# The first chunk's block squarings, with units crossed between the column halves of the matmul array

## The chip, the core and the metric

The kernel runs on one core of a Trainium2 chip. Its engines work side by side, each through its own list of instructions in a fixed order: TensorE (PE, with its weight loads shown as PEld), VectorE (DVE), ScalarE (ACT), GpSimd (POOL) and SyncE (SP), which issues most DMAs. The metric is the device time of one execution in microseconds (us). Before the change three runs took 644.02, 644.89 and 645.16 us; the median is 644.89.

## What is computed

A recurrent attention block (RWKV7, 4 batches, 8 heads, 768 steps, head dimension 40) and behind it a feed-forward block with an exact GELU:

```python
for t in range(S):
    y[:, :, t] = np.einsum('bhd,bhde->bhe', rt, state)
    Sa = np.einsum('bhde,bhe->bhd', state, at)
    state_decay = state * wt[:, :, None, :] - np.einsum('bhd,bhe->bhde', Sa, bt)
    state = state_decay + np.einsum('bhd,bhe->bhde', vt, kt)
...
h = x @ w_in
g = 0.5 * h * (1.0 + erf(h * inv_sqrt2))
return g @ w_out
```

x is the attention's output, 3072 rows of 320; w_in is 320 x 2048 and w_out 2048 x 320, both given in 64 bits and turned into fp32 on the chip.

## The kernel before

The sequence is cut into 12 chunks of 64 steps. Within a chunk the recurrence becomes matrix products per head: N (from a and b), A, RV, M, and the inverse of (1 - N), with which the vectors sa of all 64 steps come out at once; the state is handed from chunk to chunk by new_state. The feed-forward block of a chunk (ph, gelu, po) follows some chunks later. All instructions are put down by hand, in one order per engine; there is no scheduler. Calls of the helper keep and warm put matmuls between a constant and the identity ahead of others, to keep PE busy.

The inverse of a 64 x 64 triangular matrix is made from its two 32 x 32 diagonal blocks and a corner. For chunks from the second on, the blocks are inverted by an elimination on POOL (eliminate: 31 steps of a multiply and an add). For chunk 0 they are inverted on PE: with Z the two diagonal blocks and T = 1 + Z, each step squares Z and adds Z² T to T, so that T = (1 + Z)(1 + Z²)(1 + Z⁴)... There are five steps, k = 0 to 4; step 0 only squares, step 4 only makes the last product for T.

A unit is one head of one batch; 16 units stand on the free axis for each half of the 128 partitions, so 32 units in all, each with two blocks. Z, T and Z's transpose ZT lie in SBUF, partition half q holding unit (q, m). square(k, h) multiplies the units m of half h (8 of them, for both partition halves): the matmul of unit (q, m) reads rows half(q) of the array and writes PSUM partitions half(q), that is columns half(q) of the array. One matmul of fp32 shows in the trace as two records. A step then needs, for each h: turn_square (DVE transposes the new Z out of PSUM into ZT), copy_square (ACT copies the new Z to SBUF) and add_square (DVE adds the product Z² T to T in SBUF). Z and T are parts of one SBUF tile called SM in the trace, ZT lies in the tile Nb. Two engines that read or write one PSUM tile are kept apart by semaphores, also where both only read.

Around the squarings, in each engine's order:

- POOL: start_T(0), scale_k(0), the preparation of chunk 1's elimination, then that elimination (its tiles are called st and spare_x).
- PE: square(0, ·), flip_r, flip_k (transposes of r and k; flip_k needs scale_k), square(1, ·), square(2, 0), make_A, square(2, 1), square(3, ·), flip_v, square(4, ·), make_av, make_RV, corner_direct (the product J), joined_direct, make_saT, make_sa, make_M, make_A of chunk 1, make_QY.
- DVE: the transposes and adds, and between them mask_A and parts of the conversion of the feed-forward weights (U[..].a, m, b).
- ACT: the copies, and between them copy_r, copy_k and copy_v; copy_v needs flip_v.

QY of chunk 0 gives the state after it (new_state, DVE) and the outputs (scale_y).

## Time and profile before

| | |
|---|---|
| median of three runs | 644.89 us |
| the profiled execution | 643.49 us, its span 641.8 us |
| PE busy | 624.2 us |
| DVE, ACT, POOL busy | 450.5, 373.5, 392.2 us |
| squares of chunk 0 | from 26.2 to 46.6 us |
| granted TensorE clock | 0.996 of full speed |

The page gives busy times of one execution; a row of a timeline has the start and the length in us, then engine, line, operation, the tile written and those read, the shape and the count of merged instructions. In brackets stands the idle time of the engine ahead of the row, and what ended it. "issue" is idle time that ended with nothing that the profile shows. A table by stage has, for each stretch, its length and the busy time of each engine. The chain of waits of the whole span goes 86% through PE, so that a delay of PE's early work counts as far as nothing later waits for something else.

### The profile page before, as it was taken

How to read it: one execution, taken by the hardware profiler on the slowest of the kernel's cores; microseconds unless marked ns; L12 is line 12 of the kernel's file. 1: busy time of each engine (PE TensorE's matmuls, PEld its weight loads, DVE VectorE, ACT ScalarE, POOL GpSimd, SP SyncE). 2: the span in 40 equal slices, each digit the busy share in tenths (PEclk: the TensorE clock that was granted, in tenths of full speed). 3: DMA queues.
4: the chain of work that ended last, by engine and by line, in shares of the span. 5: the costliest groups of instructions: out<-in, count | busy, mean ns of one | idle time of the engine just before them, and what ended most of it. 6: DMA issues, size and time to landing. Idle time of an engine off the chain costs nothing.

```text
span 641.8 us, 32951 instructions
## 1 busy us (share of the span) xinstructions
PE 624.2 (97%) x14788; PEld 553.9 (86%) x14788; DVE 450.5 (70%) x604; ACT 373.5 (58%) x717; POOL 392.2 (61%) x806
## 2 busy tenths in 40 slices
PE   6899899999999999999999999999999999999997
PEld 4787788787878899998998998988989989989977
DVE  1775889996467899685995995985987965623313
ACT  4437694664265479447487587576587687274020
POOL 7587478822857814898848858858758768620000
PEclk9999899999999999999999999999999999999999
DMA  9986767448234643465555466374465450210100
GB/s 139 176 143 138 131 137 164 104 106 149 60 75 75 117 99 67 94 113 120 111 105 100 95 116 115 74 130 86 80 120 106 84 98 5 43 25 10 35 2 21
DMA packets 227119, 60.47 MB, mean 94 GB/s; under 512 B 208603, under 2 KB 225275, under 8 KB 226978
## 3 DMA queue, kind: packets, MB, share of 16 engines
q1 hardware_dynamic: 225946, 56.33, 47.2%
q8 instruction: 116, 1.90, 1.3%
q0 software_dynamic: 592, 1.70, 1.2%
q10 hardware_dynamic: 440, 0.33, 0.2%
q14 instruction: 25, 0.20, 0.1%
HBM read 50.46 MB, written 3.93 MB: 85 GB/s over the span
## 4 chain that ended last, share of the span: by engine, by line
PE 86%; DVE 4%; POOL 3%; SPq 2%; DMA 2%; ACT 2%; issue 1%; ACTq 0%; DVEq 0%; POOLq 0%
PE ph L1414 33%; PE po L1317 22%; PE QY L139 7%; PE po L1424 5%; PE po L1250 2%; PE J L139 2%; PE N_ps L139 2%; PE RV_ps L139 2%; PE saT_ps L139 2%; PE M_ps L139 2%; POOL st L863 2%; POOL st L861 2%; PE A_ps L139 1%; PE X L139 1%; PE av L139 1%
## 5 line engine op out<-in xcount | busy, mean ns | idle before, releaser
L1414 PE MATMUL ph<-xt,w_in_sb 64*64 64x256 f32 (+1 forms) x3360 | 218.4, 377 | 1.9 <-issue 1.8
L1414 PEld LDWEIGHTS ph<-xt,w_in_sb 64*64 64x64 f32 (+1 forms) x3360 | 175.1, 141 | 30.1 <-DMA v_pairs<-in_v_dram 1.7
L861 POOL TENSOR_TENSOR tmp<-W,Nb 128x126 f32<-128x126 f32 (+22 forms) x310 | 129.5, 418 | 57.6 <-DVE Nb L876 34.1
L863 POOL TENSOR_TENSOR W<-W,tmp 128x126 f32<-128x126 f32 (+22 forms) x310 | 147.3, 475 | 24.3
L1418 ACT ACTIVATE gt<-ph 128x1024 f32<-128x1024 f32 x48 | 49.2, 1025 | 92.4 <-PE ph L1414 89.0
L1317 PE MATMUL po<-w_out_sb,gt 128*128 128x160 f32 x576 | 84.3, 302 | 0.0
L1317 PEld LDWEIGHTS po<-w_out_sb,gt 128*128 128x128 f32 x576 | 79.2, 190 | 1.2
L1218 ACT COPY turned<-within 8x64 f32<-8x64 f32 (+3 forms) x144 | 46.4, 322 | 3.5 <-DVE within L1207 1.6
L814 POOL TENSOR_TENSOR VR<-VR,upper 128x1024 f32<-128x1024 f32 x8 | 18.9, 2366 | 30.2 <-ACT VR L810 26.7
L580 ACT COPY part<-part 32x256 f32<-32x256 f32 (+1 forms) x112 | 36.1, 322 | 1.7
L1424 PE MATMUL po<-w_out_sb,gt 128*128 128x320 f32 x128 | 36.5, 438 | 0.5 <-DVE w_out_sb L386 0.5
L1092 DVE STREAM_TRANSPOSE sa<-saT 128x1024 f32<-128x1024 f32 x9 | 11.1, 1238 | 32.1 <-ACT saT L1079 32.1
L1101 ACT COPY SM<-sa 32x64 f32<-32x64 f32 (+1 forms) x108 | 31.8, 294 | 1.4
L1424 PEld LDWEIGHTS po<-w_out_sb,gt 128*128 128x128 f32 x128 | 23.7, 190 | 10.2 <-DVE w_out_sb L386 1.0
L1340 DVE TENSOR_TENSOR os<-os,po 128x160 f32<-128x160 f32 x63 | 19.7, 314 | 17.4 <-PE po L1317 10.5
L1337 ACT COPY os<-po 128x160 f32<-128x160 f32 x9 | 2.6, 290 | 41.9 <-PE po L1317 41.9
L376 ACT ACTIVATE conv<-conv,rebias 128x320 uint32<-128x320 uint32 (+1 forms) x26 | 15.8, 620 | 15.7 <-DVE conv L373 15.6
L1317 PE MATMUL po<-extra,half 128*128 128x160 f32 x160 | 23.2, 299 | 0.0
L876 DVE STREAM_TRANSPOSE Nb<-N 128x1024 f32<-128x1024 f32 x10 | 21.6, 2158 | 1.7 <-ACT N L798 1.7
L1035 DVE COPY Tt<-J 32x512 f32<-32x512 f32 x9 | 6.2, 689 | 23.2 <-PE J L139 23.2
L1317 PEld LDWEIGHTS po<-extra,half 128*128 128x128 f32 x160 | 22.2, 190 | 0.0
L1317 PE MATMUL po<-extra,gt 128*128 128x160 f32 x144 | 21.1, 300 | 0.0
(301 smaller groups left out, 1280.7 us busy)
## 6 DMA issues: line engine op xcount, KB each, us to landing
VR<-in_v_dram SPq DMA_DIRECT2D x24, 160.0 KB
out_dram<-os SPq DMA_DIRECT2D x45, 80.0 KB
b_rows<-in_b_dram SPq DMA_DIRECT2D x22, 160.0 KB
k_rows<-in_k_dram SPq DMA_DIRECT2D x22, 160.0 KB
a_pairs<-in_a_dram SPq DMA_DIRECT2D x18, 144.0 KB
v_pairs<-in_v_dram SPq DMA_DIRECT2D x36, 72.0 KB
r_pairs<-in_r_dram SPq DMA_DIRECT2D x36, 72.0 KB
a_pairs<-in_b_dram SPq DMA_DIRECT2D x16, 144.0 KB
```

The source lines that it names most:

```text
L139: nc.tensor.matmul(o, lhsT, rhs, start=first, stop=True, skip_group_check=True)
L580: nc.scalar.copy(to[at:at + BL, :, x, z * BL:end], tmp[on:on + BL, e, :, q * BL:q * BL + end - z * BL])
L861: eng.tensor_tensor(t, W[:, :rows, j:j + 1].to_broadcast([P, rows, rest]), Nb[:, j:j + 1, j + 1:].to_broadcast([P, rows, rest]), ALU.mult)
L863: eng.tensor_tensor(W[:, :rows, j + 1:], W[:, :rows, j + 1:], t, ALU.add)
L876: nc.vector.transpose(Nb.rearrange("p s t -> p t s"), N[:, :, :BL].rearrange("p n t -> p t n").unsqueeze(2).to_broadcast([P, BL, 2, NBL]))
L1101: copy(SM[to:to + BL, g].rearrange("p q m c -> p (q m) c")[:, :, d * BL:end], t["sa"][at:at + BL, :, to:to + end - d * BL])
L1218: nc.scalar.copy(tn[to:to + deep, :, at:at + wide], within[0][at:at + deep, :, to:to + wide])
L1317: nc.tensor.matmul(self.pt[at][:, n, :DM // 2], l_[:, f], r_[:, f], start=f == 0, stop=f == NF // 2 - 1)
L1340: nc.vector.tensor_tensor(to, one_, other, ALU.add)
L1414: nc.tensor.matmul(pt[to:end, x, s], w_in_sb[half(x), kt, p * P + to:p * P + end], xt[half(x), kt], start=kt == 0, stop=kt == NK - 1)
L1418: nc.scalar.activation(gt[:, 4 * q:4 * q + 4].rearrange("p (x s) t -> p x s t", x=2), phs.pop((c, q)), ACT.Gelu)
L1424: nc.tensor.matmul(pos[c][:, g], gt[:, f, g * P:(g + 1) * P], w_out_sb[:, f], start=f == 0, stop=f == NF - 1)
```

## The change

In square(k, h) with k below 4, odd units n of a half now write the other half of the columns: the matmul of unit (q, m) reads rows half(q) and writes half(1 - q). So an odd unit stands in the other partition half after every such step, and after four steps is back. Its product is laid out by n % 2 over the two PSUM banks of the tile instead of by n // 4. T must follow: start_T puts the odd units' T into the other half to begin with, in eight operations instead of four; add_square adds T from SBUF to the product in PSUM, one operation for the even units and one for each half of the odd ones; copy_square copies Z and T (96 columns instead of 64) to SBUF, behind the adds. In step 3, where no copy_square for Z is wanted, add_square itself has ACT copy T. In step 4 everything is as before. In the list of calls one add_square and one copy_square change places.

```diff
     def start_T(c, eng):
-        for rows, cols in quads:
-            eng.tensor_tensor(sq["T"][rows], sq["Z"][rows, :, cols], ident[rows, rows].unsqueeze(1).to_broadcast([BL, NBL, BL]),
-                              ALU.add)
+        for x in range(2):
+            for n, (rows, cols) in enumerate(quads):
+                to = quads[(n + 2 * x) % 4][0]
+                eng.tensor_tensor(sq["T"][to, x::2], sq["Z"][rows, x::2, cols],
+                                  ident[rows, rows].unsqueeze(1).to_broadcast([BL, NBL // 2, BL]), ALU.add)
 
     def square(k, h):
         at, end = 0 if k < 4 else HP, HP if k == 0 else 3 * BL
         pt = duo("sq", 2 * k + h)[:, :, :12 * BL].rearrange("p z (n t) -> p z n t", t=3 * BL)
-        sq["pt", h] = pt
+        sq["pt", h], sq["k", h] = pt, k
         for n in range(NBL // 2):
             for q in range(2):
-                m = h * NBL // 2 + n
-                mm(pt[half(q), n // 4, n % 4, at:end], sq["ZT"][half(q), m], sq["both"][half(q), m, at:end])
+                m, to = h * NBL // 2 + n, half(q ^ n % 2 if k < 4 else q)
+                mm(pt[to, n % 2, n // 2, at:end], sq["ZT"][half(q), m], sq["both"][half(q), m, at:end])
 
     def halves(t, h):
-        return t[:, h * NBL // 2:(h + 1) * NBL // 2].rearrange("p (z n) t -> p z n t", z=2)
+        return t[:, h * NBL // 2:(h + 1) * NBL // 2].rearrange("p (n z) t -> p z n t", z=2)
 
     def copy_square(h):
-        nc.scalar.copy(halves(sq["Z"], h), sq["pt", h][:, :, :, :HP])
+        end = 3 * BL if sq["k", h] else HP
+        nc.scalar.copy(halves(sq["both"], h)[:, :, :, :end], sq["pt", h][:, :, :, :end])
 
     def add_square(h):
-        T = halves(sq["T"], h)
-        nc.vector.tensor_tensor(T, T, sq["pt", h][:, :, :, HP:], ALU.add)
+        T, pt, k = halves(sq["T"], h), sq["pt", h][:, :, :, HP:], sq["k", h]
+        if k == 4:
+            nc.vector.tensor_tensor(T, T, pt, ALU.add)
+            return
+        nc.vector.tensor_tensor(pt[:, 0], T[:, 0], pt[:, 0], ALU.add)
+        for q in range(2):
+            nc.vector.tensor_tensor(pt[half(q), 1], T[half(1 - q), 1], pt[half(q), 1], ALU.add)
+        if k == 3:
+            nc.scalar.copy(T, pt)
...
     turn_square(1)
     load_w(2)
+    add_square(1)
     copy_square(1)
-    add_square(1)
     substitute(1, 8)
```

## Prediction, made before the changed kernel was run

> **What bounds the kernel now.** The page first, then the waits of the stretch behind the change, then a table by stage.

> ```profile
> span 641.8 us, 32951 instructions
> PE 624.2 (97%) x14788; PEld 553.9 (86%) x14788; DVE 450.5 (70%) x604; ACT 373.5 (58%) x717; POOL 392.2 (61%) x806
> ...
> DVE st L1187 <- PE QY L139: 2.7, 1, 2.7
> ...
> 70.00:80.00 10.00, 10.00 (x318) 7.99 (x317) 9.90 (x17) 6.86 (x10) 4.62 (x4) 0.98 0.49 116
> 80.00:90.00 10.00, 9.04 (x346) 7.84 (x346) 9.41 (x13) 9.55 (x16) 6.69 (x8) 1.00 0.48 125
> 90.00:130.00 40.00, 39.50 (x798) 32.97 (x795) 37.53 (x65) 23.79 (x32) 33.67 (x69) 1.00 0.65 137
> ```

> In the table by stage the third number is PE's busy time, then PEld, DVE, ACT, POOL. From 70 us on DVE (9.90 of 10, 9.41 of 10, 37.53 of 40) and then PE have no room; DVE came to that backlog after 2.7 us of waiting for QY of chunk 0 (matmuls that end near 69.7 us). So whatever moves that QY moves the end about one for one. QY hangs, in PE's fixed order, on the corner product J of chunk 0, and J on the block squarings: the change lies on the chain, though it touches only 26 to 50 us.

> **The matmuls alone.** From the timeline of PE (start, length, count):

> ```profile
> 25.18 1.16 PE L139 MATMUL N_ps<-aT,nT 40*64 40x64 f32 x64
> 26.16 2.03 PE L139 MATMUL sq<-SM,Nb 64*64 64x64 f32 x64
> 31.04 2.86 PE L139 MATMUL sq<-SM,Nb 64*64 64x96 f32 x64
> 44.51 2.00 PE L139 MATMUL sq<-SM,Nb 64*64 64x32 f32 x62
> 101.20 1.66 PE L139 MATMUL QY<-SM,extra 64*64 64x104 f32 x64
> ```

> N_ps is written in just the order of halves that the squares get (rows and columns 0/0, 1/1, 0/1, 1/0) and needs 1.16 us for 64 records of 64 columns; the squares of today, on 0/0 and 1/1 only, need 2.03. QY, on all four, needs 1.66 for 104 columns, the squares 2.86 for 96. I take 1.43 for a pair of squares with 96 columns, 0.71 for a half of it: 0.72 off each half, 1.0 off step 0, nothing off step 4, which isn't crossed. Bounds: 0 (no gain) and 0.72.

> **Ahead of the squares: POOL.**

> ```profile
> 23.08 5.25 POOL L931 TENSOR_TENSOR SM<-SM,ident 32x512 f32<-32x512 f32 x4 [9.54 <-ACT wpT L527]
> 28.41 1.56 POOL L626 TENSOR_TENSOR extra<-k_rows,part 128x640 f32<-128x640 f32 x1
> 30.02 0.86 PEld L587 LDWEIGHTS kT_ps<-ident,extra 128*128 128x128 f32 x8 [0.29 <-POOL extra L626]
> 31.29 0.24 POOL L861 TENSOR_TENSOR st<-st,spare_x 128x31 f32<-128x31 f32 x1 [0.45 <-DVE spare_x L876]
> 47.30 0.41 POOL L861 TENSOR_TENSOR st<-st,spare_x 128x126 f32<-128x126 f32 x1
> ```

> start_T goes from four operations of 512 elements (5.25/4 = 1.31 each) to eight of 256. Through 0.41 plus a gap of some 0.04 at 126 elements and 1.31 at 512, 256 cost 0.74: 5.9 us in all, +0.65; bounds 0 (cost by elements alone) and +1.3 (twice that). Four of them cross partitions, which no row shows; the upper bound is for that. scale_k follows on POOL, PE's kT transposes wait for it (the 0.29), and squares 1 follow these on PE. So step 0's gain of 1.0 is lost in that wait, and square(1,0) starts at 31.7 instead of 31.04. POOL's own elimination for chunk 1 had 0.45 to spare and starts 0.2 later; its result is turned on DVE behind masks that PE holds up anyway.

> **Inside the squares: DVE and ACT.**

> ```profile
> 32.63 0.72 DVE L947 STREAM_TRANSPOSE Nb<-sq 128x512 f32<-128x512 f32 x1 [1.49 <-PE sq L139]
> 33.27 0.38 DVE L954 TENSOR_TENSOR SM<-SM,sq 128x256 f32<-128x256 f32 x1
> 33.58 0.41 DVE L373 TENSOR_SCALAR conv<-w_out_sb 128x512 uint32<-128x512 uint32 x1
> 35.78 0.42 DVE L954 TENSOR_TENSOR SM<-SM,sq 128x256 f32<-128x256 f32 x1 [1.12 <-ACT SM L950]
> 37.06 1.21 DVE L755 TENSOR_TENSOR A<-A_ps,upper 128x1024 f32<-128x1024 f32 x1
> 39.26 0.41 DVE L954 TENSOR_TENSOR SM<-SM,sq 128x256 f32<-128x256 f32 x1
> 40.37 0.72 DVE L947 STREAM_TRANSPOSE Nb<-sq 128x512 f32<-128x512 f32 x1 [0.71 <-ACT SM L950]
> 41.32 0.42 DVE L954 TENSOR_TENSOR SM<-SM,sq 128x256 f32<-128x256 f32 x1 [0.23 <-PE sq L139]
> 41.66 0.71 DVE L947 STREAM_TRANSPOSE Nb<-sq 128x512 f32<-128x512 f32 x1
> 46.83 0.41 DVE L954 TENSOR_TENSOR SM<-SM,sq 128x256 f32<-128x256 f32 x1
> ...
> L1340 DVE TENSOR_TENSOR os<-os,po 128x160 f32<-128x160 f32 x63 | 19.7, 314 | 17.4 <-PE po L1317 10.5
> ...
> 33.76 0.58 ACT L950 COPY SM<-sq 128x512 f32<-128x512 f32 x1 [2.83 <-DVE SM L954]
> 39.76 0.58 ACT L950 COPY SM<-sq 128x512 f32<-128x512 f32 x1 [1.92 <-DVE SM L954]
> 44.63 1.01 ACT L727 COPY vT<-vT_ps 128x1024 f32<-128x1024 f32 x1 [4.29 <-PE vT_ps L139]
> 80.15 0.38 ACT L1009 COPY Js<-J 128x256 f32<-128x256 f32 x1
> ```

> An add of 256 elements takes 0.41, one of 160 takes 0.314: 1 ns per element and 0.15 fixed, so 128 take 0.28. Below step 4 each add becomes three of 128 elements, each waiting for the end of the one before (0.03): 0.93 for 0.41. Bounds 0.61 (half of 0.41 each, no gap) and 1.05 (0.314 each). No row has DVE writing to PSUM; the upper bound stands for it. ACT's copies grow from 64 to 96 columns: between 0.58 at 512 elements and 1.01 at 1024 (which are the bounds), 768 cost 0.80; and they must now wait for the adds. In step 3 ACT gets two new copies of T of 256 elements (0.38, as Js).

> Now the chain, before → after, each event started by the last thing it waits for:

> - Square(1,0) seen by DVE: 32.63 → 32.55 (31.7 + 0.71 + 0.15 to DVE).
> - DVE then runs without a pause: transpose 0.7, adds 0.93, the conversion 0.4, transpose, adds (36.25), transpose and adds of step 2 (37.95). mask_A, 37.06 → 37.95. The 1.12 that DVE waited for ACT are used up by it. Add(1) of step 2 follows the same conversions: 39.26 → 40.2, end 39.67 → 41.1.
> - Copy(1), 39.76 → 41.2, now 0.80: the transpose behind it 40.37 → 42.05.
> - Add(0) of step 3 stands behind that transpose on DVE: 41.32 → 42.8, end 43.75. Transpose(0) waits for the new copy of T (43.85 to 44.25), since two engines take turns at one PSUM tile: 41.66 → 44.3.
> - flip_v needs that transpose (its PSUM tile): 42.61 → 45.05, and copy_v 44.63 → 47.05. The copy of T(1) stands behind copy_v on ACT, 48.05 to 48.45; transpose(1) waits for it, ends 49.15, and square(4,1) starts then instead of 45.5 (half of the 2.00).
> - Behind the copy of T(1) ACT also holds the conversion of a weight unit, wanted on DVE only after add(1). Add(1) of step 4: 46.83 → 50.4. On PE av, RV and a warming matmul follow square(4,1), and J starts at 52.5 instead of 49.45.

> ```profile
> 42.61 1.97 PE L139 MATMUL vT_ps<-ident,VR 128*64 128x128 f32 x32
> 48.06 0.89 PEld L139 LDWEIGHTS RV_ps<-rT,vT 40*64 40x64 f32 x52 [0.45 <-issue]
> 49.45 1.20 PE L139 MATMUL J<-Nb,N 32*32 32x32 f32 x64
> 52.63 0.14 PEld L587 LDWEIGHTS rT_ps<-ident,v_pairs 128*128 128x128 f32 x1 [0.83 <-issue]
> 56.63 0.20 PEld L139 LDWEIGHTS saT_ps<-Tt,avs 64*64 64x64 f32 x7 [0.20 <-issue]
> 60.36 0.32 PEld L139 LDWEIGHTS M_ps<-rT,saT 40*64 40x64 f32 x15 [0.32 <-issue]
> 66.28 0.46 PEld L139 LDWEIGHTS QY<-SM,extra 64*64 64x64 f32 x18 [2.31 <-issue]
> ...
> q8 instruction: 116, 1.90, 1.3%
> ```

> So +3.05 us at J; the 0.45 in RV is used up in it. Had the adds cost 0.61, the same steps give +1.4 at J, because the new copy of T behind copy_v stays. What then lies between J and QY are the "issue" gaps. Queue 8, of kind instruction, moved 116 packets: 2 x 14788 instructions over them is 255 each, so 128 weight loads and 128 matmuls; and the gaps stand about 128 records apart (52 of RV, 2, 64 of J, 2, 7 of rT up to 52.63). [...] They go by when PE enters the block before, so most of the delay passes; with light DMA traffic at the new times I take 0.55 of the 0.83 and the smaller ones off: **+2.5 us at QY**, and at the end. The profiled execution took 643.49 (span 641.8 and 1.7 around it): 646.0. It lies 1.4 below the median of the runs, 644.89; on that the forecast is **647.4**.

> [...]

> **The rivals.**

> [...] Chance 0.22: 0.13 that it ends within 0.2%, 0.09 faster. [...]

> *The permuted transposes are slow* (slower still). One row stands for it:

> ```profile
> 62.62 1.12 DVE L892 STREAM_TRANSPOSE Nb<-st 128x512 f32<-128x512 f32 x1
> ```

> 1.12 instead of 0.71 for the same 512 elements, where the order is permuted finely; L949 keeps runs of 64, so I don't expect it; six transposes on the chain would add 2.4: 649.8. Chance 0.07.

> *The crossing gives PE nothing*: only square(1,0) is on the chain as a matmul, so +0.7: 648.1. N_ps speaks against it. Chance 0.06.

> **How the numbers follow.** My forecast (delay passes, 645.7 to 648.6 as adds and POOL go from bound to bound: +1.4 or +4.3 at J, less 0.55) has 0.65. Changes under 0.2% (1.3 us) can't be told from none. Slower: 0.65 + 0.07 + 0.06, less 0.02 for cheap adds within the forecast: 0.76. Same: 0.13 + 0.02 = 0.15. Faster 0.09. The range, 644.0 to 649.4, leaves out most of the faster half of the first rival and the slow transposes.

> **What would show it.** Squares 1 to 3 at 1.4 us per 64 records; three DVE operations of about 0.28 per add, DVE busy nearly without a pause from 32.5 to 41; ACT copies of 0.80; copy of T(1) behind copy_v; J near 52.5 and QY's second part near 68.8. Wrong: J at or before 49.5, or J late and QY at 66.3.

## The result, and the profile after

The changed kernel took 650.42 us (median of four runs: 646.82 to 653.02) against 644.45 us before (the three runs given above and a fourth of 641.05): ratio 1.011, 95% interval 1.0075 to 1.0146. In a second set of six runs (after_again below) it was 1.0103 (1.0065 to 1.0141). It is slower by about 1%, 6 us between the medians and 7 by the ratio, where +2.5 was forecast; the time lies outside the forecast range of 644.0 to 649.4.

The profiled execution after took 651.02 us. The page's span, and the table by stage (length, then busy time of PE, PEld, DVE, ACT and POOL, the granted TensorE clock, DMA share, GB/s):

```profile
span 649.3 us, 32970 instructions
```

```profile
10.00:20.00 10.00, 6.81 (x60) 5.35 (x64) 1.23 (x1) 5.78 (x6) 3.54 (x6) 0.81 1.27 186
20.00:26.00 6.00, 6.00 (x74) 5.88 (x67) 2.96 (x3) 1.08 (x2) 0.00 (x0) 0.50 1.18 144
...
32.00:40.00 8.00, 4.74 (x115) 3.97 (x113) 6.09 (x11) 4.49 (x7) 6.78 (x18) 1.00 1.02 177
40.00:47.00 7.00, 6.97 (x129) 4.99 (x128) 5.69 (x13) 2.45 (x4) 5.90 (x15) 0.51 0.89 124
...
70.00:80.00 10.00, 9.80 (x227) 8.49 (x229) 6.12 (x9) 5.33 (x10) 3.55 (x3) 0.66 0.11 20
```

The last number but two, the granted clock, had no term in the prediction: TensorE ran at half clock at 16 to 26, at 40 to 47 and at 71 to 78 us. The first of these lies ahead of every changed instruction on TensorE; the start of start_T on POOL, which nothing of the change precedes, moved from 23.08 to 26.45. So the chain has to be read from start_T on. From its timeline, one engine after the other:

```profile
26.45 6.20 POOL L933 TENSOR_TENSOR SM<-SM,ident 32x256 f32<-32x256 f32 x8 [12.92 <-ACT wpT L527]
35.35 1.55 PE L139 MATMUL sq<-SM,Nb 64*64 64x96 f32 x64
43.31 2.93 PE L139 MATMUL sq<-cum_m,ident 128*128 128x512 f32 x4
49.71 1.97 PE L139 MATMUL vT_ps<-ident,VR 128*64 128x128 f32 x32 [1.34 <-DVE Nb L949]
57.27 1.20 PE L139 MATMUL J<-Nb,N 32*32 32x32 f32 x64
...
36.31 0.72 DVE L949 STREAM_TRANSPOSE Nb<-sq 128x512 f32<-128x512 f32 x1 [1.25 <-PE sq L139]
37.13 0.30 DVE L960 TENSOR_TENSOR sq<-SM,sq 128x128 f32<-128x128 f32 x1
37.53 0.70 DVE L962 TENSOR_TENSOR sq<-SM,sq 64x128 f32<-64x128 f32 x2
38.33 0.43 DVE L373 TENSOR_SCALAR conv<-w_out_sb 128x512 uint32<-128x512 uint32 x1
...
44.80 0.29 DVE L960 TENSOR_TENSOR sq<-SM,sq 128x128 f32<-128x128 f32 x1
45.13 0.63 DVE L962 TENSOR_TENSOR sq<-SM,sq 64x128 f32<-64x128 f32 x2
46.70 0.72 DVE L949 STREAM_TRANSPOSE Nb<-sq 128x512 f32<-128x512 f32 x1 [0.94 <-ACT SM L953]
...
45.87 0.80 ACT L953 COPY SM<-sq 128x768 f32<-128x768 f32 x1 [2.58 <-DVE sq L962]
48.53 0.37 ACT L964 COPY SM<-sq 128x256 f32<-128x256 f32 x1 [1.86 <-DVE sq L962]
51.72 1.01 ACT L727 COPY vT<-vT_ps 128x1024 f32<-128x1024 f32 x1 [2.82 <-PE vT_ps L139]
52.63 0.38 ACT L964 COPY SM<-sq 128x256 f32<-128x256 f32 x1
```

What the crossing should do it does: 64 records of 96 columns fell from 2.86 to 1.55 us. What it costs is there too: eight operations of 0.775 on POOL, three sums in the place of one (37.13 to 38.23, later 44.80 to 45.76), copies of 0.80, and the copy of T(1) at 52.63, right behind copy_v. From the start of start_T to J is 57.27 - 26.45 = 30.82 us, and 49.45 - 23.08 = 26.37 before: **+4.45**, where the prediction had +3.05. This distance is used for all kernels below. In the first profile before it is 26.37; in four further profiles of kernels that leave the squarings as they were (before_again, before_warm_early, shift_24, shift_64) it is 25.88 to 26.44, so that a figure from one profile is good to about half a microsecond.

### The profile page after: what moved, and what is told of

Read it like the earlier page. It is cut to its first block, busy times and chain, and to the rows that moved or that the text cites. A ratio compares the mean times of both kernels' runs of the same rounds, so it can differ in the third digit from the quotient of the medians.

```text
span 649.3 us, 32970 instructions
## 1 busy us (share of the span) xinstructions
PE 627.5 (97%) x14788; PEld 555.5 (86%) x14788; DVE 453.4 (70%) x616; ACT 375.1 (58%) x719; POOL 395.7 (61%) x810
## 4 chain that ended last, share of the span: by engine, by line
PE 89%; DVE 3%; ACT 2%; issue 1%; POOL 1%; SPq 1%; DMA 1%; DVEq 0%; ACTq 0%; POOLq 0%
PE ph L1424 33%; PE po L1327 22%; PE QY L139 7%; PE po L1434 5%; PE J L139 3%; PE po L1260 2%; PE A_ps L139 2%; PE M_ps L139 2%; PE saT_ps L139 2%; PE N_ps L139 2%; PE RV_ps L139 2%; PE av L139 2%; PE X L139 1%; PE sq L139 1%; SPq L194 1%
## 5 line engine op out<-in xcount | busy, mean ns | idle before, releaser
L863 POOL TENSOR_TENSOR W<-W,tmp 128x126 f32<-128x126 f32 (+22 forms) x310 | 151.0, 487 | 24.3
L861 POOL TENSOR_TENSOR tmp<-W,Nb 128x126 f32<-128x126 f32 (+22 forms) x310 | 129.1, 416 | 57.4 <-DVE Nb L876 33.9
L1350 DVE TENSOR_TENSOR os<-os,po 128x160 f32<-128x160 f32 x63 | 19.7, 313 | 17.4 <-PE po L1327 10.5
L876 DVE STREAM_TRANSPOSE Nb<-N 128x1024 f32<-128x1024 f32 x10 | 21.6, 2156 | 1.7 <-ACT N L798 1.7
L755 DVE TENSOR_TENSOR SM<-M_ps,upper 128x1024 f32<-128x1024 f32 x12 | 14.7, 1223 | 11.4 <-PE M_ps L139 11.2
```

Source lines behind the costliest of these rows:

```text
L861: eng.tensor_tensor(t, W[:, :rows, j:j + 1].to_broadcast([P, rows, rest]), Nb[:, j:j + 1, j + 1:].to_broadcast([P, rows, rest]), ALU.mult)
L863: eng.tensor_tensor(W[:, :rows, j + 1:], W[:, :rows, j + 1:], t, ALU.add)
L876: nc.vector.transpose(Nb.rearrange("p s t -> p t s"), N[:, :, :BL].rearrange("p n t -> p t n").unsqueeze(2).to_broadcast([P, BL, 2, NBL]))
L1350: nc.vector.tensor_tensor(to, one_, other, ALU.add)
```

## The experiments

**Both kernels again, and the stretch ahead of the change.** before_again and after_again are the two kernels unchanged. The two others have four warming products more, ahead of cum of the second chunk:

```diff
+    warm(4, 4, 4, 4)
     sums_cum(1)
```

> The kernel before, unchanged, once more, for the spread of its time and of its granted clock. Theory (clock): the stretch of half clock at 15.4 to 25.7 us in the profile of the changed kernel (0.50 granted, wT_ps 128x128 x16 3.78 us against 2.05) stands ahead of every changed instruction, behind an idle TensorE stretch that both kernels have (3.0 us before cum, behind ACT wpT L527); so it is a matter of the execution and not of the change, and the kernel before has it in some executions too: its executions lie in two groups, near 641 to 642 us with a mean clock of 0.996 or more, and near 645 us with a clock of 0.988 to 0.99. Rival (the change makes it): the kernel before never has it; all its executions have a clock of 0.995 or more.

> The kernel before with four warming products of 512 columns (about 0.64 us each by the row of N_ps<-cum_m,ident 128x512, 2.6 us together) in the idle stretch of 3.0 us ahead of cum of the second chunk. Theory (clock): full clock at 15 to 26 us in every execution, 0 to 2 us faster than before (the early dip happens in some executions only), median 642.5 to 644.5. Rival: the dip never happens in the kernel before, so nothing is gained; 644.0 to 646.5, the warming products delaying cum by up to 0.5 us.

> The changed kernel with the same four warming products in the idle stretch ahead of cum of the second chunk, nothing else. Theory (clock): the half clock at 15 to 26 us is gone in every execution; the profile shows square(0) starting near 26.2 us as before and the time falls from 650.4 to 646.5 to 648; what is left over the kernel before, 2.5 to 4 us, is the crossing's own. Rival (the early half clock is a cause of nothing, or comes from the change by another way): 649.5 or more.

> The changed kernel, unchanged, beside the three others, to have more than four executions of it. Chain of sums and copies plus a clock that varies: 648 to 650 us, clocks from 0.982 to 0.992, and the early half clock (15 to 26 us, ahead of every changed instruction) in some of the executions only. If the change makes that early stretch, every execution has it: clock never above 0.990, 650 us or more.

Measured: before_again 0.9991 (0.9968 to 1.0015), before_warm_early 0.9996 (0.9972 to 1.0021), after_warm_early 1.0081 (1.005 to 1.0112), after_again 1.0103. The kernel before has the early half clock too, here in its second profile:

```profile
10.00:20.00 10.00, 6.62 (x64) 5.26 (x68) 1.23 (x1) 5.89 (x6) 3.54 (x6) 0.87 1.27 188
...
24.50 5.23 POOL L931 TENSOR_TENSOR SM<-SM,ident 32x512 f32<-32x512 f32 x4 [10.96 <-ACT wpT L527]
...
50.47 1.20 PE L139 MATMUL J<-Nb,N 32*32 32x32 f32 x64
```

So the first stretch belongs to the execution, not to the change; and in after_wide_warming below, a form of the changed kernel, start_T starts at 23.09, with no half clock ahead of it. But the executions of the kernel before do not fall into two groups, as theory had it; in this set, with those that ran beside it, they spread from 639.45 to 647.39 us. And the warming products gained nothing that can be told, in either kernel; after_warm_early, at 649.12 us, stayed above the 646.5 to 648 expected and below the 649.5 of its rival. Its profile shows what took the place of the early half clock:

```profile
22.92 6.18 POOL L933 TENSOR_TENSOR SM<-SM,ident 32x256 f32<-32x256 f32 x8 [9.40 <-ACT wpT L527]
55.04 1.20 PE L139 MATMUL J<-Nb,N 32*32 32x32 f32 x64
```

That is 32.12 us from start_T to J, 1.30 more than in the first profile after. Half clock came at 31.1 to 34.5 us, on flip_k's transposes (1.69 us for 1.09) and the squares of step 1 (2.55 for 1.55). It came again at 38 to 45, beside VectorE's row as in the first profile after.

**The parts of the change.** uncrossed keeps all the costs and takes the crossing out; cross_only has the crossing without its costs (its sums join halves of different blocks, so that the inverse is another); three kernels put one cost each into the kernel before.

```diff
 # uncrossed, against the changed kernel
-                to = quads[(n + 2 * x) % 4][0]
+                to = rows
...
-                m, to = h * NBL // 2 + n, half(q ^ n % 2 if k < 4 else q)
+                m, to = h * NBL // 2 + n, half(q)
-            nc.vector.tensor_tensor(pt[half(q), 1], T[half(1 - q), 1], pt[half(q), 1], ALU.add)
+            nc.vector.tensor_tensor(pt[half(q), 1], T[half(q), 1], pt[half(q), 1], ALU.add)
...
 # cross_only, against the changed kernel (start_T as before)
-        end = 3 * BL if sq["k", h] else HP
+        end = HP
+        nc.vector.tensor_tensor(T, T, pt, ALU.add)
...
 # split_start_T, against the kernel before
+        for x in range(2):
+            for rows, cols in quads:
+                eng.tensor_tensor(sq["T"][rows, x::2], sq["Z"][rows, x::2, cols],
...
 # three_sums, against the kernel before (k < 4)
+        nc.vector.tensor_tensor(T[:, 0], T[:, 0], pt[:, 0], ALU.add)
+        for q in range(2):
+            nc.vector.tensor_tensor(T[half(q), 1], T[half(q), 1], pt[half(q), 1], ALU.add)
...
 # one_sum_in_psum, against the kernel before (k < 4; copies of 96 columns behind it)
+        nc.vector.tensor_tensor(pt, T, pt, ALU.add)
+        if k == 3:
+            nc.scalar.copy(T, pt)
```

> The changed kernel with the crossing alone taken out: every unit stays in its half of the columns, while start_T keeps its eight operations, every sum its three operations into PSUM, ScalarE its copies of 96 columns and the copies of T in step 3. The squares of 96 columns go back to 2.86 us for 64 (now 1.55). Theory (clock): TensorE is busy longer between the waits, the granted clock stays at 1.00 at 32 to 47 us, and the mean clock is 0.993 or more against 0.985 of the changed kernel; so the kernel that does more work on TensorE is the faster one of the two, 645.5 to 648.5 us. Rival (chain): 0.71 us more in each half of a square adds to the chain of sums and copies; 651 to 654 us.

> The crossing alone: squares on four tiles, with four operations in start_T, one sum of 128 partitions into T and copies of 64 columns, as in the kernel before. T stays on its own side, so each sum joins the halves of two different blocks: the inverse is not the reference's. Theory (clock): the squares shrink from 2.86 to 1.5 us for 64, nothing else grows, and the time is still not under that of the kernel before, since TensorE idles more than a third of 31 to 42 us and the clock falls to 0.5 for some microseconds behind it: mean clock 0.985 to 0.992, 644 to 648 us. Rival (the sums and copies alone make the loss): J starts 1 to 3 us earlier than before (before: 49.45 us), 641 to 643 us.

> The kernel before with start_T alone in eight operations of 256 elements instead of four of 512, as the changed kernel has them (every one of the changed kernel took 0.775 us: 6.20 for 5.25). Nothing else is changed; the result is the reference's. Theory (the sums and their copies make the loss): flip_k's transposes start 1 us later (31.0 for 30.02), the lead of TensorE is lost but VectorE has 1.1 us of waiting for ScalarE behind it, so J starts 0.3 to 1 us later, and the time is that of the kernel before within 1 us: 643.5 to 645.5. Rival (POOL's operations make a large part): 646 or more.

> The kernel before with each sum of steps 1 to 3 in three operations of 128 elements a partition, still into T in SBUF; start_T, copies and matmuls as before. Theory (VectorE's row is the bound from 32.6 to 41 us): a sum takes 1.05 to 1.15 us for 0.41; four of them stand in the row between the first transpose (32.63) and the end of the last sum of step 2 (39.67), which had 0.6 us of waiting, so that end comes 2.0 to 2.4 us later, and J 2.5 to 3 us; the time rises to 646 to 648. Rival (VectorE has room, ScalarE's copies set the pace): J within 1 us of before, 643.5 to 645.

> The kernel before with the sums of steps 1 to 3 written into PSUM in one operation, ScalarE copying 96 columns behind them (0.80 us for 0.58) and T of step 3 by itself (0.38 each), as the changed kernel has it; no operation is split and nothing crosses. Theory (VectorE's row sets the time up to step 2): there +0.3 us a half at most, 0.5 us behind each copy of T in step 3, and 1.0 to 1.5 us where the copy of T(1) stands behind copy_v on ScalarE: J starts 2 to 3 us later, 645.5 to 648. Rival (nothing but the splitting costs): J within 1 us of before, 643.5 to 645.

Timelines of POOL and PE, uncrossed first, then cross_only:

```profile
23.26 6.18 POOL L933 TENSOR_TENSOR SM<-SM,ident 32x256 f32<-32x256 f32 x8 [9.72 <-ACT wpT L527]
54.87 1.20 PE L139 MATMUL J<-Nb,N 32*32 32x32 f32 x64
```

```profile
25.85 5.25 POOL L931 TENSOR_TENSOR SM<-SM,ident 32x512 f32<-32x512 f32 x4 [12.32 <-ACT wpT L527]
50.59 1.20 PE L139 MATMUL J<-Nb,N 32*32 32x32 f32 x64
```

And split_start_T, then three_sums:

```profile
26.74 6.17 POOL L932 TENSOR_TENSOR SM<-SM,ident 32x256 f32<-32x256 f32 x8 [13.20 <-ACT wpT L527]
54.71 1.20 PE L139 MATMUL J<-Nb,N 32*32 32x32 f32 x64
```

```profile
25.65 5.24 POOL L931 TENSOR_TENSOR SM<-SM,ident 32x512 f32<-32x512 f32 x4 [12.11 <-ACT wpT L527]
53.82 1.20 PE L139 MATMUL J<-Nb,N 32*32 32x32 f32 x64
```

| kernel | ratio to before (95%) | start_T to J, less 26.37 |
|---|---|---|
| split_start_T | 1.0028 (1.0006 to 1.0051) | +1.60 |
| three_sums | 1.0053 (1.0033 to 1.0073) | +1.80 |
| one_sum_in_psum | 1.0058 (1.0029 to 1.0088) | (J fell into a half clock) |
| uncrossed: all three | 1.0111 (1.0075 to 1.0146) | +5.24 |
| cross_only | 0.9982 (0.9953 to 1.001) | -1.63 |

Each cost by itself makes the kernel slower; together they make as much as the whole change. The crossing alone brings J 1.63 us forward and 0.18% at the end, which can't be told from nothing. So the chain theory was right on uncrossed (652.27 us) and the clock theory, which had it faster than the changed kernel, wrong. On cross_only the clock theory missed too: the mean clock of its twelve executions is 0.995, as before, not 0.985 to 0.992; its J came forward as the rival had it, and its time, 643.47 us, lies between the rival's 643 and the theory's 644. My sizes for the single parts missed: split_start_T, at 647.11 us, fell to its rival (646 or more). POOL's own part of its +1.60 is 0.92 us, and TensorE waited 0.41 us more in square(2,1) and 0.20 more in RV with nothing that the profile shows ("issue"). three_sums came out at J at less (1.80 for 2.5 to 3), though its time, 647.84, is in the range; one_sum_in_psum, at 648.54, lies just above its range of 645.5 to 648.

**TensorE kept busy.** after_warm_all adds warming products at five places, eight products more; after_wide_warming and after_moved_warming keep the count of products, and only widen or move products that are there:

```diff
 # after_warm_all: the four early products, then
-    keep(1)
+    keep(4, 2)
     flip_k(0)
-    keep(1)
+    keep(4, 4)
     square(2, 0)
...
+    warm(4, at=2)
     flip_v(0)
...
+    keep(4)
     square(4, 0)
...
 # after_wide_warming
-    keep(1)
+    keep(4)
     flip_k(0)
-    keep(1)
+    keep(4)
     square(2, 0)
...
 # after_moved_warming, besides
-    keep(2, 4)
     square(3, 0)
...
+    keep(4)
     square(3, 1)
+    warm(4)
     flip_v(0)
```

> The changed kernel with warming products in the early idle stretch and also in the four idle stretches among the crossed squarings: ahead of flip_k (768 columns for 128), square(2,0) (1024 for 128), flip_v (512) and square(4,0) (512). Theory (clock): the half clock at 40 to 47 us (A_ps 1.99 us, 32 squares of 96 columns 1.50 us, four warming products 2.93 us) goes too; J starts near 52.5 us, where the chain of the adds alone puts it, and the time is 1 to 3 us under that of the changed kernel with the early products only. Rival (chain): TensorE's clock there is hidden behind VectorE and ScalarE, so the time stays within 0.7 us of that kernel, or grows by the products that come late.

> The changed kernel with the warming product ahead of flip_k and the one ahead of square(2,0) of 512 columns instead of 128; the number of TensorE instructions is the same, so nothing moves in its stream. Together they put 1.0 us more of work into the idle stretches of 1.4 and 1.9 us. Theory (clock): the half clock at 40 to 47 us goes, the mean clock rises by 0.003 to 0.006, and the time falls by 1 to 2.5 us against after_again. Rival (chain): VectorE's row sets J whatever the clock does there; J within 0.3 us of where the changed kernel has it behind its own start of start_T (30.8 us later), and the time within 0.8 us of after_again.

> after_wide_warming with the two warming products ahead of square(3,0) moved into the two idle stretches behind it: one of 512 columns ahead of square(3,1) (idle 2.5 us) and one of 512 ahead of flip_v (idle 1.3 us); the number of TensorE instructions stays. Theory (clock on the chain): flip_v's transposes take 1.97 us again (3.35 in after_wide_warming), J stands 4.3 to 4.8 us later than before behind the same start of start_T (5.72 there), and the time is 1 to 3 us under after_wide_warming. Rival (the dip only moves to another place of the chain, av, RV or QY): J at +5.5 or more, time unchanged within 1 us.

Measured: after_warm_all 1.0184 (1.0152 to 1.0217), far outside both expectations; a later run bears on it. after_wide_warming 1.0117 (1.0079 to 1.0156), no better than after_again beside it (652.79 for 653.30 us): in time the rival was right. Its J was not, 32.08 us behind start_T for 30.8. The row of VectorE up to the end of step 2 took 9.33 us for 9.45 in the first profile after, so TensorE doesn't set the pace there; but the half clock came at 46.6 us instead and fell on flip_v. after_moved_warming 1.0089 (1.0055 to 1.0123). The timelines of after_again, after_wide_warming and after_moved_warming:

```profile
26.18 6.19 POOL L933 TENSOR_TENSOR SM<-SM,ident 32x256 f32<-32x256 f32 x8 [12.64 <-ACT wpT L527]
49.66 3.29 PE L139 MATMUL vT_ps<-ident,VR 128*64 128x128 f32 x32 [1.33 <-DVE Nb L949]
58.06 2.01 PE L139 MATMUL RV_ps<-rT,vT 40*64 40x64 f32 x62
60.73 1.49 PE L139 MATMUL J<-Nb,N 32*32 32x32 f32 x48
```

```profile
23.09 6.21 POOL L933 TENSOR_TENSOR SM<-SM,ident 32x256 f32<-32x256 f32 x8 [9.56 <-ACT wpT L527]
46.24 3.35 PE L139 MATMUL vT_ps<-ident,VR 128*64 128x128 f32 x32 [1.33 <-DVE Nb L949]
55.17 1.20 PE L139 MATMUL J<-Nb,N 32*32 32x32 f32 x64
```

```profile
24.39 6.19 POOL L933 TENSOR_TENSOR SM<-SM,ident 32x256 f32<-32x256 f32 x8 [10.85 <-ACT wpT L527]
47.51 1.97 PE L139 MATMUL vT_ps<-ident,VR 128*64 128x128 f32 x32 [0.28 <-DVE Nb L949]
54.98 1.20 PE L139 MATMUL J<-Nb,N 32*32 32x32 f32 x64
```

flip_v's transposes take 1.97 us at full clock and 3.3 at half, and copy_v, the copy of T(1) and square(4,1) stand behind them. With the idle time ahead of flip_v filled (0.28 left of 1.33), they took 1.97 again, and J came 30.59 us behind start_T: +4.22, about what the first profile after has (+4.45), whose half clock at 40 to 47 lay off the chain. Where a half clock lay on the chain it was +5.71 (wide), +5.75 (warm_early) and +8.18 (again, with av, RV and J in it too). The mean of the five is +5.66. In time the filled gap gave nothing that can be told (651.48 for 652.79 us, each beside a set of its own of the kernel before; the intervals of the two ratios overlap).

**The copy of T(1) ahead of copy_v:**

```diff
     flip_v(0)
-    copy_v(0)
     U[0].m()
     add_square(1)
+    copy_v(0)
```

> after_moved_warming with copy_v put behind the second sum of step 3 on ScalarE, so that the copy of T(1) doesn't stand behind copy_v. Theory (the chain as predicted, with T(1) behind copy_v at 50.5 for 47.5 us): the transpose of that half starts some 2.5 us earlier, square(4,1) follows copy T by 1 us, J stands 2 to 3 us earlier than in after_moved_warming, and the time falls by 1.5 to 3 us, to within 0.5% of the kernel before. Rival (RV's products, which need copy_v, set J): J at most 1 us earlier, time the same within 1 us.

Measured 1.0051 (1.0016 to 1.0085), 648.06 us. ScalarE's timeline, then J:

```profile
47.73 0.37 ACT L964 COPY SM<-sq 128x256 f32<-128x256 f32 x1 [2.16 <-DVE sq L962]
48.38 1.01 ACT L727 COPY vT<-vT_ps 128x1024 f32<-128x1024 f32 x1 [0.29 <-PE vT_ps L139]
```

```profile
23.25 6.18 POOL L933 TENSOR_TENSOR SM<-SM,ident 32x256 f32<-32x256 f32 x8 [9.71 <-ACT wpT L527]
...
52.88 1.20 PE L139 MATMUL J<-Nb,N 32*32 32x32 f32 x64
```

J lies 29.63 us behind start_T, +3.26: only 0.96 earlier than in after_moved_warming, not 2 to 3, so that for J the rival was right (av and RV then set it). Its time fell by 3.4 us against after_moved_warming, to 0.51% over the kernel before, as the theory had it; but the two intervals overlap, and 0.96 us at J doesn't explain 3.4. It is the fastest of the forms with the reference's result in which units cross and the count of instructions is kept, and still slower than the kernel before.

**Sums on TensorE, and a place in the stream.** Two kernels let TensorE add T into PSUM, with products of the identity:

```diff
+        if 0 < k < 4:
+            for z in range(2):
+                for q in range(2):
+                    mm(pt[half(q ^ z), z, :, HP:], ident[half(q), half(q)], halves(sq["T"], h)[half(q), z], False)
...
 # cross_steps_1_2: the same for k in (1, 2); start_T and the sums of steps 3 and 4 as before
-                m, to = h * NBL // 2 + n, half(q ^ n % 2 if k < 4 else q)
+                m, to = h * NBL // 2 + n, half(q ^ n % 2 if k in (1, 2) else q)
...
 # shift_24, in the kernel before (shift_64: 24 here, 40 ahead of sums_cum(1))
     sums_cum(0)
+    pt = duo("warm", 0)
+    for n in range(24):
+        mm(pt[half(0), n % 2, :4], ident[half(0), half(0)], ident[half(0), :4])
```

> The changed kernel with the sums of steps 1 to 3 made by TensorE: behind each half of a square four products of the identity's 64x64 blocks with T (128 columns each, side by side on four tiles; estimate 0.3 us from kT_ps 128x128, 0.28 us) add T into PSUM, VectorE does no sum there, ScalarE copies 96 columns as now. start_T keeps its eight operations. Theory (clock and chain): VectorE loses three operations (1.05 us) per half, J starts 2 to 4 us earlier than in the changed kernel, mean clock 0.988 to 0.995, 645 to 648 us. Rival (neither the sums nor the clock are the cause, but ScalarE's copies of 0.80 us and POOL's 0.9 us): 649 us or more.

> Crossed in steps 1 and 2 only, with the sums of these two steps on TensorE as in the run beside it; steps 0, 3 and 4, start_T (four operations) and the sums of steps 3 and 4 (one operation into T) as in the kernel before. All units are back on their side behind step 2, so that no copy of T is needed. Theory (clock and chain): TensorE has 1.43 + 0.6 us per step for 2.86, VectorE 0.82 us less per step; square(3,0) starts 1 to 2 us earlier than in the kernel before; the clock stays above 0.992; 641.5 to 644.5 us. Rival (any crossing idles TensorE enough to lose the clock): mean clock below 0.991, 645 to 648 us.

> The kernel before with 24 products of 64x64 with 4 columns behind cum of the first chunk, where TensorE waits for a_pairs (8.0 to 10.3 us); each is about 0.03 us, 0.7 in all, and nothing reads them. They only push every later TensorE instruction 48 places on in the stream that it is fed from. Theory (the two kernels with sums on TensorE lost 20 us by where the borders between the fetched blocks of instructions fall, not by their products): 655 us or more, with issue waits of 1 to 2.5 us all along the span, as those two had (N_ps 4.1, J 3.4, QY 2.3, X 2.2 us). Rival (the place in the stream costs nothing; the products into PSUM do): 643 to 645.5 us.

> The kernel before with 64 products of 64x64 with 4 columns that nothing reads: 24 at the place of shift_24 and 40 in the idle stretch ahead of cum of the second chunk. Each gives two matmul records in the trace (shift_24: 24 products, 48 records), so 64 move the stream by 128 records, one whole block. Theory (place in the stream modulo 128 records): back to 643 to 647 us, though there are more than twice as many added products as in shift_24. Rival (each added product costs): 675 us or more.

> sum_on_TensorE with 40 of the same idle products ahead of the squarings, so that its 24 products of the sums and these 40 make 64: from step 3 on every instruction has its old place modulo 128 records. Theory (place in the stream, and VectorE's row): the 20 us are gone; J starts about 0.6 us later than before behind the same start of start_T (it did in sum_on_TensorE) and the time is 643.5 to 647, under the changed kernel by 3 us or more. Rival (sums on TensorE cost by themselves): 655 us or more.

Measured: sum_on_TensorE 1.033 (1.0289 to 1.0371), cross_steps_1_2 1.0305 (1.0259 to 1.0351), shift_24 1.0256 (1.0213 to 1.03), shift_64 1.0049 (1.0017 to 1.0081), sum_on_TensorE_in_place 1.0066 (1.0034 to 1.0098). No theory had foreseen the first two: the first lies in its rival's range (649 or more), but 16 us above the bound and not by the rival's cause. The waits of shift_24, TensorE's alone (total, count, longest):

```profile
PE J L139 <- issue: 4.1, 3, 1.8
PE N_ps L139 <- issue: 3.4, 2, 2.0
PE X L139 <- issue: 2.2, 1, 2.2
PE saT_ps L139 <- issue: 2.0, 1, 2.0
```

The longest in shift_64:

```profile
PE M_ps L139 <- issue: 1.2, 1, 1.2
```

24 products that nothing reads, 2.96 us of TensorE in all, cost 17 us; 64 of them, which move the stream by 128 records, cost 3 to 4 (over the 643 to 647 us expected, far under the rival's 675), although they make start_T 7.6 us late. TensorE's "issue" waits over the whole span add up to 5.6 us before and 5.3 in shift_64, but to 16.3 in shift_24, 17.1 in sum_on_TensorE and 16.3 in cross_steps_1_2. So it is the place of the instructions in TensorE's stream that costs, not the number of products. The other 6 us or so of shift_24 go with half clock, of which its six executions had more (mean clock 0.985 for 0.995 before). In after_warm_all these waits are 6.7 us for 3.7 in the first profile after: that is at most half of the 6.8 us that it lies above after_warm_early, and the rest isn't explained.

Up to J, sum_on_TensorE shows what VectorE's sums are worth:

```profile
25.47 6.18 POOL L933 TENSOR_TENSOR SM<-SM,ident 32x256 f32<-32x256 f32 x8 [11.94 <-ACT wpT L527]
52.42 0.62 PE L139 MATMUL J<-Nb,N 32*32 32x32 f32 x27
```

J started 26.95 us behind start_T: +0.58, for +4.45 in the changed kernel, where VectorE makes these sums. In time that was not to be had: sum_on_TensorE_in_place, with 12 and 28 of the idle products ahead of the squarings, missed both its theory (643.5 to 647 us) and its rival (655 or more). Only the instructions from step 3 on have their old place there; the squares themselves met such waits, and J was at +4.61:

```profile
PE sq L139 <- issue: 3.9, 2, 2.2
```

## Why the prediction was wrong

- *Squares 1 to 3 at 1.43 us*: right, a little small (1.55 by the row; cross_only has J earlier by 1.63).
- *start_T +0.65, square(1,0) at +0.66*: too small. The operations took 0.775 for 0.74, and square(1,0) started 35.35 - 26.45 = 8.90 us behind start_T for 31.04 - 23.08 = 7.96: +0.94. By itself the splitting costs 0.28% (split_start_T).
- *From the first square seen by DVE to the end of add(1) of step 2, 32.55 to 41.1*: 8.55 predicted, 36.31 to 45.76 = 9.45 measured. This is the larger part of the term that was mis-sized. In after_warm_early, after_again and after_wide_warming the same stretch took 9.39, 9.25 and 9.33. The first sum took 1.10 and the others 0.96 for 0.93; about 0.1 us passes between each transpose and the sum behind it (37.03 to 37.13), for which I gave nothing; and from the end of the first sum to the next transpose, with the conversion of L373 between them, it is 0.55 us (38.23 to 38.78) for the 0.4 that I gave.
- *From there to J*: 11.4 predicted, 57.27 - 45.76 = 11.51 measured. The waits behind the new copies of T, copy_v and T(1) came as described, nearly to the tenth. after_copy_T_first shows that the last of these waits is worth 1 us.
- So "+3.05 us at J" is +4.22 to +4.45 at full clock.
- *The granted clock* was no term of the sum at all. Shorter squares and longer work on VectorE together leave TensorE idle between 32 and 54 us (busy 4.74 us of 8.00 at 32 to 40 in the first profile after, for 7.92 before), and half clock follows (from 40.07); neither alone did it in the profiles of cross_only and uncrossed (6.39 and 6.81 of 8.00), which have none between 24 and 67 us. Where it meets flip_v, the squares of step 1 or the products up to J it adds 1.3 to 3.7 us. With it J is +5.66 in the mean of five profiles (the first after, after_again, after_warm_early, after_wide_warming and after_moved_warming).
- *0.55 off behind J*: no run shows this term, and it can't be told. From J to the end of the span it is 592.3 and 593.5 us in the two profiles of the kernel before, and 592.0, 594.5, 592.8, 591.2, 589.7 and 589.4 in the changed kernel and its forms (first, again, wide, moved, warm_early, copy_T_first), a spread of 5 us. In the two profiles of the changed kernel itself no gain shows. That the gaps absorb the delay is neither borne out nor refuted. TensorE's "issue" gaps between J and QY are 2.88 and 3.16 us in the two profiles before; they are 2.59 in the first profile after, but 0.50 in after_again, where J comes latest. So there they did shrink, by over 2 us, and yet after_again has 594.5 us from J to the end. What the trace of before shows of them: the five from RV to QY (0.45, 0.83, 0.20, 0.32 and 2.31 us) end 1.41 to 1.52 us behind the landing of a packet of 16384 bytes of queue 8 (the last at 66.28, for 64.76), and the next packet starts 1.12 to 3.02 us behind the end of each. That such a packet takes longer beside loads is not shown: the 116 packets took 0.88 to 1.70 us, and this time hardly goes with the share that the other queues were busy meanwhile (correlation 0.10). That most of the delay passes was the author's estimate. The delay at the end agrees with it; the shrinking gaps of after_again and shift_24's 16.3 us of such waits do not.
- *The rivals of slow transposes and of a crossing that gives nothing* fell: 0.72 us for each transpose, 1.55 for the squares. But in cross_only, squares in about half the time (1.55 us for 2.86) gained nothing at the end that can be told: 0.9982.

+5.66 at J, if it passes whole, comes near the 6 to 7 us measured; five single profiles, three of them of altered kernels, are no proof of it. The direction, the queue of waits and the place of each were right. Wrong were the size of VectorE's row (and with it the 3.05) and that the clock was left out; the 0.55 taken off is not shown by any run. That half clock makes up the difference between the +4.2 to +4.45 and the +5.66 is shown by the rows of flip_v, of the squares of step 1, of RV and of J; that filling the gaps gains it back in time is not shown (0.9% left, the intervals overlap).

How the measured loss divides between chain and clock stays open. Over 127 executions of the kernel before (in before_again and in the sets beside the other runs), time and mean granted clock go together, about 0.6 us for each 0.001 of clock. The ten of the changed kernel have 0.9835 in the mean, for 0.995 before. At that rate the clock alone would make 6.9 us, the whole of the loss, while the chain at full clock makes 4.2 to 4.45. The two can't simply be added, since a half clock beside VectorE's row (40 to 47 us in the first profile after) delays nothing up to J. Against the clock as the only cause stands uncrossed: at a mean clock of 0.992 it is as slow as the changed kernel (1.0111). So the added operations cost about 7 us without the crossing, and what the crossing gains on the chain is gone again in the changed kernel, with its lower clock.

## What to carry to other kernels

Before packing small matmuls tighter, price what the packing makes dearer on the engines that empty PSUM: here the packing was worth 1.6 us of the chain and nothing that can be told at the end, and the extra operations on POOL, VectorE and ScalarE that it needed cost 7 us (uncrossed). Add up a row that runs without a pause with every small operation in it, since what stood in its idle time before now counts (9.45 us here from the first square seen to the end of add(1) of step 2, where 8.55 was predicted); and after a change that idles TensorE, look at the granted clock behind it (0.51 here at 40 to 47 us). Compare variants only with the same number of TensorE instructions ahead of what follows (24 products that nothing reads cost 2.56% in shift_24).

## What the runs showed of the hardware

```
after          16.17 10240 0.5   40.07 6827 0.5   70.79 6827 0.5
after_again    18.29  6827 0.5   35.35 3413 0.5   49.01 3413 0.5   55.83 10240 0.5
before         66.99  3413 0.5
before_again   17.45  3413 0.5
```

A window that was busy in part was enough for the fall: after, the one at 36.65 was busy for 45%, and half clock came at 40.07; before, the one at 63.57 for 38%, and half clock came at 66.99. In the matmul records of all traces, leaving out the last 15 us of each, 27 windows at full clock were busy for 45% or less, and half clock followed each time; the least busy window behind which full clock stayed was at 46%, and up to 76% it sometimes fell too (the windows full of products of 4 columns, below, apart). It is no sharp line: in those last 15 us full clock stayed behind windows at 43% and 44% (cross_steps_1_2, after). This fits that the same idle 3.0 us ahead of cum cost the clock in some executions only: before, the grid cut it in two windows, 50% and 59% busy; after, one window was 34% busy. Products of 4 columns did not keep the clock up: two windows of shift_64 that were busy throughout, 2.06 and 3.07 of their 3.41 us with such products, were followed by half clock all the same.

The other surprise is the price of a place in TensorE's instruction stream: 48 records further on, 2.56% of the time and 10.7 us more of "issue" waits; 128 further on, 0.49% and no more of them (5.3 us for 5.6).
